# RWKV attention with a mixture of experts behind it: the first expert's weight pieces are requested by two engines in turn, and the state of six units is faded by TensorE

## The chip, the core and the metric

The kernel runs on one core of one Trainium2 chip. A core has a matrix engine (TensorE, called PE in the profile), a vector engine (VectorE, DVE), a scalar engine (ScalarE, ACT), a general engine (GpSimd, POOL), an engine that mostly issues transfers (SyncE, SP), and 16 DMA engines. PE, DVE, ACT, POOL and SP each run their own list of instructions in order and wait for one another by semaphores. The metric is the time of one execution in microseconds (us) on the chip; smaller is better.

## The reference

Attention first, for 4 batches, 8 heads, 768 tokens and a head width of 48; then a mixture of 8 experts on the 3072 tokens of 384 numbers that come out of it, each token going to the one expert with the highest logit.

```python
for t in range(S):                                   # S = 768
    kt, vt, rt = k[:, :, t], v[:, :, t], r[:, :, t]
    cur = np.einsum('bhd,bhe->bhde', u[None] * kt, vt)
    y[:, :, t] = np.einsum('bhd,bhde->bhe', rt, state + cur)
    state = w[None, :, :, None] * state + np.einsum('bhd,bhe->bhde', kt, vt)
...
logits = x @ w_gate + modality_bias[modality_id]     # x: 3072 x 384
e_idx = np.argmax(logits, axis=1)
...
for e in range(E):                                   # E = 8
    h = np.maximum(x[mask] @ w1[e], 0.0)             # 384 x 1024
    out[mask] = gate_w[mask, None] * (h @ w2[e])     # 1024 x 384
```

## The kernel before

**Units.** The attention is cut into 24 units: chunk c = 0 to 5 of 128 tokens, and in each chunk the batches b = 0 to 3; unit i is `c*4 + b`. The decay w is taken out by powers (`rc`, `kc`, `kt` are r and k multiplied by powers of w). For a unit, `scores` makes the 128x128 score blocks of the 8 heads on PE, `causal` masks them on DVE into `at`, and `values` puts into one PSUM bank `py` the product of r with the state `st` that the earlier chunks left (L396) and the product of `at` with v (L403). Into a second bank, `pst`, it puts the unit's own contribution to the state, k times v (L410), and the eight numbers per token by which v itself enters (`bonus`, L341). There is one bank for `pst`, so the next unit's L410 waits until the last reader of the bank has finished. The scales of the expert weights (`pww`, below) use the same bank.

**The state.** The state of a batch after a chunk is the state before, multiplied row by row by w to the 128th power, plus the contribution in `pst`. The multiplication is done by `fade` on ACT (L384: two 112x192 activations in a step, for two batches and half of the head pairs), into the other of two state buffers; the addition by `state` on DVE (L444: two additions in a step, for the upper and the lower half of the rows). Both are done one step apart per unit.

**The step loop.** One loop of 23 steps writes the program out by hand. Step i works on several units at a time: PE's `scores(i+1)`; DVE's `token(i-1)` (`py` plus `dv`, L418), followed by ACT's square of the row (L433); `taken(i)` (DVE copies the eight numbers to `d`); `state(i-1)`; the `begin` hooks; POOL's sends of rows (L580), `decay` (POOL `rc`, L313), `carry` (POOL `kt`, L320), DVE's `kc` (L332); the row's scale on DVE; `own(i, 0)` on ACT, four of the eight activations v times d into `dv` (L354); `high(i-1)` on ACT (L456); `causal(i+1)` on DVE (L374); `own(i, 1)` on ACT, the other four; `low(i-1)` on DVE (L460); `flip(i-1)`, a transposing transfer that SP issues (L465); `values(i)` on PE; `fade` on ACT; and the `at` hooks. POOL's `own_keys` (L325, `rk`) is written at a step's start.

Ahead of `scores(i)` for units 1 to 13 stand `DENSE` = 6 matmuls of 128x512 on constant data (L362), whose result is overwritten.

**The first expert.** Its weights (W1 and W2 together, 3 MB in float32) come in six pieces of 128x1024 (`raw`, 512 KB each, L824), all issued by SP: piece 0 at the end of step 8, 1 and 2 at the end of step 9, 3 and 4 at the end of step 10, 5 at the end of step 11. The constant `O` is 8. SP reads the expert's number with `value_load` ahead of piece 0. For each piece ACT makes the sum of squares (`norm`, L827): piece 0 at the end of step 9, pieces 1 and 2 at the end of step 10, 3 and 4 at the end of step 11, 5 at the end of step 12. From pieces 0 to 2 comes the scale of W1 (`scales("w1")`: a small PE matmul L841 into `pww`, then DVE from L844 on) at the beginning of step 11; from pieces 3 to 5 that of W2 at the beginning of step 13. `split` makes of a piece its high half in float16 on ACT (`whi`, L857) and the rest on DVE (`wlo`, L862): piece 0 at the end of step 11, 1 and 2 at the end of step 12, 3 to 5 at the end of step 13. The experts' matmuls (L916 up, L990 down) begin at the end of step 12, between the attention's; after step 23 the other experts follow.

Since every engine's list is in order, a `norm` that waits for its piece holds up all that ACT has behind it, and the PE matmul of a scale that waits for a `norm` holds up all of PE's list.

## Time and profile before

| | |
|---|---|
| three runs | 365.92, 362.83, 364.58 us; median 364.58 |
| the profiled execution | 365.14 us, of which the span from first to last instruction is 363.3 |
| PE busy | 337.2 us, 93% of the span |
| DVE, ACT, POOL busy | 230.3, 178.2, 167.2 us |
| mean granted clock of PE | 0.968 |
| mean DMA rate over the span | 138 GB/s |

The profile is a record of one execution. Times in it are microseconds from the start of the span. "L827" is line 827 of the kernel before; the kernel of the change has other line numbers, up to 32 higher. In a line of the timeline the first number is the start, the second the busy time, then the engine, the line, the operation, the tiles (out <- in), their sizes, and how many instructions were put together (x4); in square brackets stands how long the engine had been idle ahead of it and what it waited for. A record of the windows gives for a stretch of time the busy time of each engine with its number of instructions, the granted clock of PE as a share of full speed (PEclk), the mean busy share of the DMA engines, and their rate. One PE matmul of the program in float32 shows as two records.

In this kernel the steps 8 to 13 lie at about 52 to 106 us.

### The profile page before, as it was taken

To read this page: it belongs to the slowest core of one execution; us is meant where nothing else is said; L and a number is where in the kernel's file an instruction comes from. 1 tells how busy PE (TensorE), PEld (TensorE's weight loads), DVE (VectorE), ACT (ScalarE), POOL (GpSimd) and SP (SyncE) were. 2 spreads that over 40 slices of the span, in tenths; PEclk is the share of its full clock that TensorE was granted. 3 is DMA by queue.
4 is the path that set the end of the run, shared out by engine and by line. 5 is a ranking of instruction groups with operands and counts; after the bars stand their busy time and mean duration, and the time that the engine had idled before them with its cause. 6 is when DMAs were issued, how large, how long until landed. Compare 5 with 4: busy or idle time off the path is not lost. (4 is left out here: it accounts for less than half of the span.)

```text
span 363.3 us, 14983 instructions
## 1 busy us (share of the span) xinstructions
PE 337.2 (93%) x5387; PEld 265.1 (73%) x5387; DVE 230.3 (63%) x762; ACT 178.2 (49%) x479; POOL 167.2 (46%) x229
## 2 busy tenths in 40 slices
PE   7799999869799999999999899997999999999893
PEld 3577778557788787988977677775677888777661
DVE  7867999979797977596558632349432323323950
ACT  7467874778656566566432122245122222256711
POOL 7996867845436673444165511136111121111731
PEclk9899999958799999999999999999999999999998
DMA  6988997998957998863354631125922212112120
GB/s 179 270 212 167 202 241 201 296 289 180 234 124 151 215 242 258 176 133 85 87 110 153 242 69 43 43 43 164 232 65 56 52 43 62 46 22 65 22 56 5
DMA packets 60749, 50.29 MB, mean 138 GB/s; under 512 B 46872, under 2 KB 54311, under 8 KB 60448
## 3 DMA queue, kind: packets, MB, share of 16 engines
q1 hardware_dynamic: 57504, 40.21, 49.8%
q0 software_dynamic: 3200, 9.47, 7.1%
q8 instruction: 30, 0.49, 0.6%
q14 instruction: 15, 0.12, 0.1%
HBM read 28.39 MB, written 11.83 MB: 111 GB/s over the span
## 5 line engine op out<-in xcount | busy, mean ns | idle before, releaser
L916 PEld LDWEIGHTS <-whi 128*128 128x128 f16 x1248 | 73.6, 99 | 3.7 <-issue 0.9
L990 PEld LDWEIGHTS <-hh 128*128 128x128 f16 x416 | 38.0, 98 | 32.9 <-ACT hh L920 8.0
L916 PE MATMUL phb<-mxT,whi 128*128 128x128 f16 x768 | 50.8, 219 | 0.0
L354 ACT ACTIVATE dv<-kv,d 128x48 f32<-128x48 f32 x192 | 47.9, 323 | 4.8 <-DVE d L346 2.8
L325 POOL TENSOR_TENSOR rk<-rc,kc 128x512 f32<-128x512 f32 x24 | 30.6, 1275 | 40.0 <-DVE posi L554 13.5
L920 ACT ACTIVATE hh<-phb 128x256 f16<-128x256 f32 (+1 forms) x48 | 21.3, 454 | 42.0 <-PE L990 13.7
L916 PEld LDWEIGHTS <-wlo 128*128 128x128 f16 x624 | 38.2, 99 | 3.2 <-DVE wlo L862 3.2
L925 DVE SCALAR_TENSOR_TENSOR hl<-phb,hh 128x256 f16<-128x256 f32 (+1 forms) x48 | 24.2, 511 | 24.7 <-ACT hh L920 14.5
L374 DVE TENSOR_TENSOR at<-psc,mask 128x512 f32<-128x512 f32 x48 | 31.6, 683 | 4.5 <-PE psc L368 4.3
L313 POOL TENSOR_TENSOR rc<-ud,powr 128x512 f32<-128x512 f32 (+1 forms) x27 | 31.8, 1184 | 2.7 <-PE py L396 1.5
L1000 DVE TENSOR_SCALAR fac<-mt,wf 128x1 f32<-128x1 f32 x17 | 3.6, 212 | 45.5 <-ACT otb L876 39.0
L916 PE MATMUL phb<-mxT,wlo 128*128 128x128 f16 x384 | 30.0, 219 | 2.6 <-DVE wlo L862 2.6
L995 PEld LDWEIGHTS <-hl 128*128 128x128 f16 x208 | 19.3, 97 | 14.7 <-issue 3.1
L876 ACT ACTIVATE otb<-po,fac 128x384 f32<-128x384 f32 x16 | 9.2, 577 | 42.2 <-PE phb L916 42.2
L990 PE MATMUL po<-wlo,hh 128*128 128x384 f16 x136 | 28.0, 326 | 1.7 <-DVE wlo L862 1.7
L580 POOL DMA_INDIRECT rows<-row,posi x24 | 24.1, 1006 | 11.6 <-DVE base L556 3.6
L990 PE MATMUL po<-whi,hh 128*128 128x384 f16 x136 | 28.3, 327 | 1.0 <-ACT hh L920 1.0
L885 POOL TENSOR_TENSOR seenb<-otb,putb 128x1 int32<-128x1 int32 x16 | 5.0, 310 | 52.8 <-ACT otb L876 50.0
L368 PEld LDWEIGHTS psc<-rc,kc 64*64 64x64 f32 (+1 forms) x768 | 21.5, 136 | 9.8 <-issue 4.8
L916 PE MATMUL phs<-mxT,whi 128*128 128x128 f16 x432 | 28.5, 224 | 0.0
L368 PE MATMUL psc<-rc,kc 64*64 64x128 f32 (+1 forms) x768 | 27.6, 280 | 0.9 <-issue 0.7
L403 PE MATMUL py<-kv,at 128*64 128x48 f32 x768 | 28.0, 229 | 0.0
(255 smaller groups left out, 673.7 us busy)
## 6 DMA issues: line engine op xcount, KB each, us to landing
ud<-in_pd SPq DMA_DIRECT2D x24, 384.0 KB
kv<-in_pt SPq DMA_DIRECT2D x24, 384.0 KB
raw<-in_w SPq DMA_DIRECT2D x12, 512.0 KB
raw<-in_w SPq DMA_DIRECT2D x2, 1536.0 KB, 6.3
rows<-pad SPq DMA_DIRECT2D x10, 193.0 KB
rows<-row,posi POOLq DMA_INDIRECT x24
xT<-row SPq DMA_TRANSPOSE x23
xn<-rows SPq DMA_TRANSPOSE x17
```

Of the source, the lines that this page charges most:

```text
L313: nc.gpsimd.tensor_mul(u["rc"][:, s], u["rT"][:, s], self.powr[:, s])
L325: nc.gpsimd.tensor_mul(u["rk"], u["rc"], u["kc"])
L354: nc.scalar.activation(u["dv"][:, sl], u["v"][:, sl], AF.Copy, scale=u["d"][:, h : h + 1])
L368: nc.tensor.matmul(u["ps"][j][s, pr * P : (pr + 1) * P], u["kc"][r, pr, s], u["rc"][r, pr, :], start=True, stop=True)
L374: nc.vector.tensor_mul(u["at"][:, j * NPR : (j + 1) * NPR, :], u["ps"][j].rearrange("p (q t) -> p q t", q=NPR), self.mask.unsqueeze(1).to_ ...
L403: nc.tensor.matmul(py[t, sl], u["at"][:, j * NPR + pr, t], u["v"][:, sl], start=c == h == 0, stop=h == H - 1, skip_group_check=True)
L580: i = nc.gpsimd.indirect_dma_start(out=self.rows, out_offset=bass.IndirectOffsetOnAxis(ap=u["posi"][:, b : b + 1], axis=0), in_=u["row"][: ...
L916: self.nc.tensor.matmul(ph[:, q * P : (q + 1) * P], w[:, c0 : c0 + P], self.xT[:, xq, t * P : (t + 1) * P], start=i == q == 0, stop=i == l ...
L920: self.nc.scalar.activation(self.hh[:, f0 : f0 + fb, t * P : (t + 1) * P], p3, AF.Relu)
L925: self.nc.vector.scalar_tensor_tensor(self.hl[:, f0 : f0 + fb, r], p3, 0.0, self.hh[:, f0 : f0 + fb, r], ALU.max, ALU.subtract)
L990: self.nc.tensor.matmul(po[:, :DM], self.hh[:, f, t * P : (t + 1) * P], w[:, c0 : c0 + DM], start=n == q == f == 0, stop=False)
L995: self.nc.tensor.matmul(po[:, :DM], self.hl[:, f, t * P : (t + 1) * P], self.whi[:, c0 : c0 + DM], start=False, stop=f == FB - 1)
```

## The change

Four edits come together.

- **The pieces.** The even pieces are issued by SP, one at the end of each of the steps 8, 9 and 10. The odd ones are issued by ACT, one in the middle of each of the steps 9, 10 and 11 (a new hook, `mid`, behind `high` and ahead of `causal`), with a `value_load` of the expert's number on ACT ahead of piece 1. The squares are spread: 1, 3 and 5 in the middle of steps 10, 11 and 12 and 0, 2 and 4 at the end of steps 9, 10 and 11.
- **The state of units 8 to 13** (`FADED`). ACT's `fade` and DVE's two additions are left out for them. Instead PE multiplies the old state by a diagonal matrix `wd` with w to the 128th power (four float32 matmuls of 112x112 on 112x96), into the bank `pst`, and L410 adds the unit's contribution on top. ACT copies the sum out of the bank in one 112x384 copy (`settled_state`), in the next step behind the row's square. The matrices are made once, by four activations on ACT in the setup.
- **Half of d times v for units 9 to 13** (`SHARED`). The second four of ACT's eight activations become one multiplication of 128x192 on POOL.
- **Fewer constant matmuls.** Ahead of `scores` of units 9 to 13 stand two, not six.

The core of the diff:

```diff
+FADED = range(8, 14)
+SHARED = range(9, 14)
...
+        self.wd = c.tile([P, NPR, 112], F32, name="wd")
+        for pr in range(NPR):
+            nc.scalar.activation(self.wd[:112, pr, :], self.id32[:112, :112], AF.Copy, scale=self.w128[:112, pr : pr + 1])
+            yield
...
     def own(self, i, q):
+        if q and i in SHARED:
+            half = lambda t: t[:, DM // 2 :].rearrange("p (h e) -> p h e", e=D)
+            nc.gpsimd.tensor_mul(half(u["dv"]), half(u["v"]), u["d"][:, H // 2 :].unsqueeze(2).to_broadcast([P, H // 2, D]))
+            return
...
-            for q in range(DENSE):
+            for q in range(2 if i - 1 in FADED else DENSE):
                 nc.tensor.matmul(u["ps"][q % 2], self.ones16, self.warm, start=True, stop=True)
...
     def fade(self, c, bs, prs):
+        if c * B + bs.start in FADED:
+            return
...
     def values(self, i):
+        faded = i in FADED
+        if faded:
+            for pr in range(NPR):
+                nc.tensor.matmul(pst[:112, pr * 2 * D : (pr + 1) * 2 * D], self.wd[:112, pr, :], st[:112, b, pr, :], start=pr == 0, stop=False, skip_group_check=True)
...
-                nc.tensor.matmul(pst[HALVES[j], sl], u["kt"][:, pr, HALVES[j]], u["v"][:, sl], start=True, stop=True)
+                nc.tensor.matmul(pst[HALVES[j], sl], u["kt"][:, pr, HALVES[j]], u["v"][:, sl], start=not faded, stop=not faded or h == H - 1, skip_group_check=faded)
...
     def state(self, i, j):
+        if i in FADED:
+            return
...
+    def settled_state(self, i):
+        if i in FADED:
+            b, c = self.units[i]
+            self.nc.scalar.copy(self.st[(c + 1) % 2][:112, b].rearrange("p a e -> p (a e)"), self.ctx_[i]["pst"][:112, :DM])
...
+        def beside(q):
+            if q == 1:
+                self.eida = nc.scalar.value_load(self.ctl[:, :1], min_val=0, max_val=E - 1)
+            self.load(self.eida, NQ, q, eng=nc.scalar)
...
-            plan(O + (q + 1) // 2, first(q))
+            if q % 2 == 0:
+                plan(O + q // 2, first(q))
...
-        plan(O + 2, norm(1))
+        mid[O + 1] = lambda: beside(1)
+        mid[O + 2] = lambda: (beside(3), self.norm(junk, 1))
+        mid[O + 3] = lambda: (beside(5), self.norm(junk, 3))
+        mid[O + 4] = norm(5)
         plan(O + 2, norm(2))
...
-        plan(O + 3, norm(3))
         plan(O + 3, norm(4))
...
-        plan(O + 4, norm(5))
...
             each(i, self.taken) if i else None
+            each(i - 1, self.settled_state)
...
             each(i - 1, self.high)
+            mid.get(i, lambda: None)()
```

How the instructions stand on three engines, before and after. First ACT, from the end of step 9 to the beginning of step 11; `junk` is the result of a `norm`, `row,ssq` of the row's square, `row<-py,sx` of `high`. Before:

```order
L827 ACTIVATE junk,wssq<-raw 128x1024
L433 ACTIVATE row_1311,ssq_1313<-py_1363 128x384
L354 ACTIVATE dv_1486<-kv_901,d_1467 128x48 x4
L456 ACTIVATE row_1311<-py_1363,sx_1314 128x384
L354 ACTIVATE dv_1486<-kv_901,d_1467 128x48 x4
L384 ACTIVATE st_93<-st_92,w_183 112x2x96 x2
L827 ACTIVATE junk,wssq<-raw 128x1024 x2
L433 ACTIVATE row_1311,ssq_1313<-py_1507 128x384
```

The same place with the change:

```order
L850 ACTIVATE junk,wssq<-raw 128x1024
L449 ACTIVATE row_1308,ssq_1310<-py_1366 128x384
L469 COPY st_93<-pst_1391 112x384
L364 ACTIVATE dv_1485<-kv_906,d_1467 128x48 x4
L479 ACTIVATE row_1308<-py_1366,sx_1311 128x384
L847 ISA
L847 DMA raw<-in_w 128x1024
L850 ACTIVATE junk,wssq<-raw 128x1024 x2
L449 ACTIVATE row_1308,ssq_1310<-py_1505 128x384
```

Four of the eight `dv` activations and the two of `fade` have gone, and a copy out of `pst` (behind the square that stands behind piece 0's `norm`) and the request for piece 3 have come in.

SP from piece 0 to pieces 3 and 4, the ends of steps 8 to 10; `ud` and `kv` are the inputs of later units, `xT` the transposes of `flip`. Before:

```order
L824 DMA raw<-in_w 128x1024
L298 DMA ud_86<-in_pd 96x1024
L305 DMA kv_1282<-in_pt 128x2x384
L465 DMA_TRANSPOSE xT_1312<-row_1311 128x6x128
L824 ISA
L824 DMA raw<-in_w 128x1024
L824 ISA
L824 DMA raw<-in_w 128x1024
L298 DMA ud_87<-in_pd 96x1024
```

With the change:

```order
L847 DMA raw<-in_w 128x1024
L304 DMA ud_86<-in_pd 96x1024
L311 DMA kv_1283<-in_pt 128x2x384
L488 DMA_TRANSPOSE xT_1309<-row_1308 128x6x128
L847 ISA
L847 DMA raw<-in_w 128x1024
L304 DMA ud_87<-in_pd 96x1024
```

Behind the transpose stands one request, for piece 2, where there were two, for pieces 1 and 2; piece 1 is now in ACT's list.

PE in step 9, from the product with the old state into the bank `pst`, with what an instruction waits for. Before:

```order
L396 MATMUL py_1363<-st_92,rc_939 64x96 [waits DVE_49]
L396 MATMUL py_1363<-st_92,rc_939 64x96 x7
L403 MATMUL py_1363<-kv_770,at_1199 64x48 [waits DMAHW5_49]
L403 MATMUL py_1363<-kv_770,at_1199 64x48 x15
L410 MATMUL pst_1388<-kv_770,kt_89 64x48 [waits DVE_49,PE_49]
```

With the change:

```order
L408 MATMUL py_1366<-st_92,rc_944 64x96 [waits DVE_49]
L408 MATMUL py_1366<-st_92,rc_944 64x96 x7
L415 MATMUL py_1366<-kv_775,at_1198 64x48 [waits DMAHW5_49]
L415 MATMUL py_1366<-kv_775,at_1198 64x48 x15
L421 MATMUL pst_1391<-st_92,wd 112x96 [waits Activation_49]
L421 MATMUL pst_1391<-st_92,wd 112x96 x3
L426 MATMUL pst_1391<-kv_775,kt_89 64x48
```

L410 (now L426) wrote first into the bank and waited for DVE's additions of the unit before; now L421 writes first and waits for ACT's copy.

More of the change, by code (lines that the diff above doesn't have):

```diff
@@ L818, in pads, with load @@
                 tc.declare_no_dep(i.ins, group="first", reason="not the first place's rows")
-    def load(self, eid, n, *qs):
+    def load(self, eid, n, *qs, eng=None):
         for q in qs:
             sl = slice(q * 2 * WC // n, (q + 1) * 2 * WC // n)
-            self.nc.sync.dma_start(self.raw[:, sl], self.w12[bass.ds(eid, 1), :, sl].rearrange("o p c -> (o p) c"))
+            (eng or self.nc.sync).dma_start(self.raw[:, sl], self.w12[bass.ds(eid, 1), :, sl].rearrange("o p c -> (o p) c"))
     def norm(self, junk, q):
@@ L1027, in run @@
         fills = []
-        at, begin = {}, {}
+        at, begin, mid = {}, {}, {}
         def plan(step, f):
```

## The prediction

> **What bounds the kernel now.** The page first: how busy each engine is.
>
> ```profile
> span 363.3 us, 14983 instructions
> PE 337.2 (93%) x5387; PEld 265.1 (73%) x5387; DVE 230.3 (63%) x762; ACT 178.2 (49%) x479; POOL 167.2 (46%) x229
> ```
>
> PE works 337.2 of 363.3 us, so the time falls only where PE idles, where its work is slow, or where it has work that can go. Next the waits of PE between 50 and 130 us, the stretch that the change touches, longest first (total, times, longest):
>
> ```profile
> PE pww L841 <- ACT junk L827: 4.6, 1, 4.6
> PE pww L841 <- DVE st L444: 2.3, 1, 2.3
> PE pst L341 <- issue: 0.6, 2, 0.4
> ```
>
> These are the matmuls of the two scales: W1's waits 4.6 us for ACT's squares of the pieces, W2's waits 2.3 us for DVE's additions to the state, which hold the one `pst` bank; the third row is a gap of 0.4 us in step 12, used below. Then the windows, with PE's granted clock as the third number from the end:
>
> ```profile
> 61.00:67.00 6.00, 6.00 (x158) 4.91 (x156) 5.86 (x26) 3.43 (x13) 3.96 (x4) 1.00 0.89 227
> 67.00:70.00 3.00, 2.98 (x66) 2.15 (x61) 2.97 (x7) 2.64 (x9) 2.25 (x3) 1.00 1.24 215
> 70.00:72.00 2.00, 1.32 (x34) 0.86 (x32) 2.00 (x9) 1.85 (x7) 2.00 (x3) 1.00 1.00 394
> 74.00:76.00 2.00, 0.07 (x1) 0.00 (x0) 0.00 (x0) 1.27 (x3) 0.00 (x0) 0.54 1.74 232
> 76.00:78.00 2.00, 2.00 (x31) 1.97 (x30) 1.80 (x9) 1.69 (x8) 0.50 (x1) 0.50 0.71 234
> 78.00:80.00 2.00, 2.00 (x45) 2.00 (x44) 2.00 (x4) 2.00 (x8) 2.00 (x3) 0.50 0.99 393
> 80.00:82.00 2.00, 2.00 (x30) 1.43 (x29) 2.00 (x5) 1.97 (x4) 0.97 (x2) 0.50 1.05 296
> 84.00:86.00 2.00, 2.00 (x56) 1.83 (x54) 1.94 (x9) 1.30 (x6) 0.71 (x1) 0.90 0.57 121
> 94.00:106.00 12.00, 12.00 (x189) 10.73 (x188) 10.29 (x23) 8.42 (x21) 5.66 (x5) 0.72 0.88 221
> 106.00:160.00 54.00, 53.21 (x1102) 44.73 (x1100) 42.06 (x145) 32.03 (x102) 29.26 (x33) 1.00 0.82 184
> ```
>
> After each wait the clock is halved for a while: 0.50 from 76 to 82, 0.72 on the mean of 94 to 106. From 94 on PE is never idle (12.00 of 12.00, then 53.21 of 54). So the end moves by as much as W2's matmul moves, plus what PE's own work and clock do behind it. Ahead of 94 the timeline says which engine sets the pace; PE first.
>
> ```profile
> 75.93 0.16 PE L841 MATMUL pww<-wssq,onesb 128*128 128x3 bf16 x1 [4.62 <-ACT junk L827]
> 76.03 1.55 PE L396 MATMUL py<-st,rc 112*64 112x96 f32 x16
> 81.13 2.72 PE L362 MATMUL psc<-warm 128*128 128x512 f16 x6
> 85.10 0.88 PE L396 MATMUL py<-st,rc 112*64 112x96 f32 x16
> 89.36 1.51 PE L916 MATMUL phs<-mxT,whi 128*128 128x128 f16 x24
> 90.71 0.83 PE L916 MATMUL phs<-mxT,wlo 128*128 128x128 f16 x12
> 93.88 0.17 PE L841 MATMUL pww<-wssq,onesb 128*128 128x3 bf16 x1 [2.34 <-DVE st L444]
> ```
>
> The same sixteen matmuls take 1.55 us at the half clock and 0.88 at the full one, a factor of 1.76. PE is through with step 12 at 91.54 (90.71 + 0.83) and waits. DVE in the same stretch:
>
> ```profile
> 76.14 0.16 DVE L844 TENSOR_REDUCE wtotw<-pww 128x1 f32<-128x3 f32 x1 [2.55 <-PE pww L841]
> 77.52 1.30 DVE L518 TENSOR_TENSOR oh<-er,mr 128x32 f16<-128x32 f32 x1
> 83.33 0.33 DVE L444 TENSOR_TENSOR st<-st,pst 64x192 f32<-64x192 f32 x1
> 83.81 0.36 DVE L444 TENSOR_TENSOR st<-st,pst 48x192 f32<-48x192 f32 x1
> 92.49 0.55 DVE L418 TENSOR_TENSOR py<-py,dv 128x384 f32<-128x384 f32 x1
> 93.03 0.71 DVE L444 TENSOR_TENSOR st<-st,pst 64x192 f32<-64x192 f32 x2
> ```
>
> It starts with W1's scale and has no idle time to speak of up to 93.74. Before the change, then, the chain is: piece 2 lands, ACT squares it, W1's scale, 17.6 us of DVE, W2's scale, and PE from there on.
>
> **The change, part by part.** *The pieces.* ACT's squares, and SP's requests:
>
> ```profile
> 66.81 1.06 ACT L827 ACTIVATE junk<-raw 128x1024 f16<-128x1024 f32 x1 [1.77 <-DMA raw<-in_w]
> 70.16 1.00 ACT L354 ACTIVATE dv<-kv,d 128x48 f32<-128x48 f32 x4
> 71.06 0.79 ACT L384 ACTIVATE st<-st,w 112x192 f32<-112x192 f32 x2
> 72.05 1.06 ACT L827 ACTIVATE junk<-raw 128x1024 f16<-128x1024 f32 x1 [0.20 <-DMA raw<-in_w]
> 74.73 1.06 ACT L827 ACTIVATE junk<-raw 128x1024 f16<-128x1024 f32 x1 [1.53 <-DMA raw<-in_w]
> 60.80 0.38 SPq L824 DMA_DIRECT2D raw<-in_w  x1
> 67.03 0.93 SPq L824 DMA_DIRECT2D raw<-in_w  x2
> ```
>
> All three squares wait for their data. Piece 1 is requested at 67.03 now, behind a transpose; from ACT, behind `high` of step 9 and the new `value_load`, it goes out some 3 us sooner, and piece 2 has one piece less ahead of it. The request and the `value_load` stand where ACT idles (1.77 us ahead of 66.81, and the 0.79 and 1.00 of `fade` and half of `dv` go too), so they cost nothing; without that cover, their own length, under 2 us. How much sooner piece 2 lands no row shows. Lower end nothing: the DMA engines are full from 61 to 76 (shares 0.89, 1.24, 1.00), the same bytes must pass, and piece 3, now requested ahead of the squares of pieces 1 and 2 and no longer behind them, shares with piece 2. Upper end 2.7 us: piece 2 in the place of piece 1, its square at 72.05 and not at 74.73. I take half, **1.3**, since 61 to 67 moved 227 GB/s and 70 to 72, almost only pieces, 394: the early stretch has some room, but not all of it.
>
> On this place bears a rule of the Trainium skill, page "DMA: Bandwidth & Descriptors", section "Issuing engines are not separate DMA queues": transfers from different engines run on the same 16 DMA engines, and issuing from several saves only the time of issuing. By it piece 2 would land as before, and this term be about nothing, as in rival 2 below; the shares near 1.00 agree.
>
> *State off DVE.* Two additions (0.33 + 0.36) leave step 12; those at 93.03 too. W2's matmul then waits for ACT: square of the row, copy. Rows for these:
>
> ```profile
> 93.12 0.49 ACT L433 ACTIVATE row<-py 128x384 f16<-128x384 f32 x1 [2.37 <-issue]
> L167 ACT COPY wtok<-pwk 128x384 f32<-128x384 f32 x1 | 0.5, 478 | 1.5 <-PE pwk L166 1.5
> ```
>
> So 0.49 + 0.48 + 0.1 for the accumulator behind `token` where it was 0.15 + 0.71: +0.2. DVE's side of W2 moves by -1.3 - 0.7 + 0.2 = -1.8. Queued behind that copy on ACT are `dv` and `high`, at most 0.5 us later, with idle time there. In step 10 the copy out of the bank stands behind the square of piece 0, which ends at 67.96; with the row's square the bank is free at about 69.0, where L410 of that step ran at
>
> ```profile
> 67.60 0.85 PE L410 MATMUL pst<-kv,kt 128*64 128x48 f32 x16
> ```
>
> PE then idles 1.4 us there; that comes out of the 4.6 us it waits later, as does whatever the four setup activations and the earlier steps shift, as long as W1's scale stays later than about 72.
>
> *Half of `dv` on POOL.* A multiplication of half the size of POOL's `kt`, so 0.6 us each.
>
> ```profile
> 77.50 1.27 POOL L325 TENSOR_TENSOR rk<-rc,kc 128x512 f32<-128x512 f32 x1 [4.53 <-DVE mr L515]
> 90.26 1.22 POOL L320 TENSOR_TENSOR kt<-kv,wtok 128x384 f32<-128x384 f32 x1
> ```
>
> In step 12 it ends at 91.48 + 0.6 = 92.1, ahead of `token` at 92.49: hidden, with 0.4 to spare; without cover, 0.6. Beside POOL's `rk` a small DVE operation took 1.30, so I add +0.3 to DVE for two more such multiplications (ends 0 and 1.2). DVE's side: **-1.5**.
>
> *PE's own work.* `wd` adds eight records in a unit where L396 has sixteen: 0.44 at the full clock, 0.8 at the half one (up to half as much again for the wider weights). The four constant matmuls that go save 1.8 us in step 12 (4/6 of 2.72). In steps 8 to 11 they make gaps that end in the wait.
>
> *The clock.* From 76 to 82 PE was 2.00 of 2.00 busy with small float32 matmuls and stayed at 0.50; it came back (0.90 at 84 to 86) after the six at 81.13. With two, I take it to stay halved until the next large float16 run, the expert's L916. The Trainium skill, page "TensorE: Matmul & The Clock Gate", Part 1, says a busy window of about 3.4 us lifts the halving whatever the instructions. By it the cut costs nothing and rival 1 would come out. Six busy microseconds at 0.50 speak against it.
>
> PE's side of W2, then: from 91.54, -1.3 (W1 sooner), -1.8 (constants), +0.8 + 0.8 (`wd` of units 11 and 12), +5.1 for the work between the clock's return and 91.54 (0.90 on the mean of 84 to 86 puts the return at 84.4; 7.1 us less the gap of 0.4 are 6.7, at a factor of 1.76), -0.9 if L916 lifts the clock midway (half of 2.34 x 0.76): 94.2. That is later than DVE's 92.4, so W2's matmul comes at 94.2, **+0.3**, without a wait ahead of it. With no wait there is no second halving: 94 to 106 at a clock of 0.72 lost 12 x 0.28 = 3.4 us; I take back **2.4**, since the first may reach into it. `wd` of unit 13: **+0.4**. Sum +0.3 - 2.4 + 0.4 = **-1.7**. From the profiled 365.14 (span 363.3 and 1.84 around it) that is 363.4; the median of the three runs is 0.56 below that execution, so the forecast is **362.9**.
>
> **Rivals.**
> 1. *The clock comes back as before*, from two constant matmuls. For it: the two still are 0.9 us of large work. W2 is then set by DVE at -1.5, the wait and the second halving remain, +0.8 for `wd`: -0.7, 363.9.
> 2. *The pieces land no sooner.* For it: the full shares. Then 1.3 of the forecast is lost: 364.2.
> 3. *Neither long halving*: W1's wait split in two gaps (1.4 and about 2) and W2's wait gone. Against it: PE idles from 71.3 (1.32 busy from 70 on), and 74 to 76 is at 0.54, so about 3 us of idleness were enough for a drop, hardly more than a gap of this rival. It would give rival 1 with the 3.4 back: -4.1, 360.5.
> 4. *Slower: the halved clock holds through step 13.* If L916's 36 matmuls do not lift it, W2 comes at 95.1 (+1.2) and step 13 runs halved as before with +0.8 for `wd`: +2.0, 366.6. It decides at L916 of step 12; one more halved stretch of the same kind behind it (half of 3.4) gives 368.3.
>
> That the change does not do what it says is possible for the requests alone: the copy that ACT runs ahead of them waits for `token`. That is rival 2.
>
> **How the numbers follow.** Forecast 0.38, rival 1 0.20, rival 2 0.14, rival 3 0.15, rival 4 0.13. A measurement can tell about 1%, 3.65 us. Below 360.9: rival 3, a tail of 0.05 of the forecast with piece 2 at its upper end (1.4 more): 0.20. Above 368.2: the further stretch of rival 4 and a price of POOL's contention at its end: 0.07. The rest, 0.73, is within. The range reaches from rival 3 with a little left out, 360.0, to rival 4, 366.8.
>
> **What would show it.** Piece 2's square ahead of 74.7 and W1's matmul at 73 to 75 (first term). No DVE additions in steps 9 to 14, the bank released by ACT. The clock between 84 and 90 at 0.50 (forecast) or near 1.00 (rivals 1 and 3), and the wait ahead of W2's matmul gone or not. POOL's `dv` ahead of `token` in step 12; if `token` waits for POOL, that term is wrong. The forecast fails if W1's matmul comes later than 76, or if the clock stays halved past 98.

## The result: 0.6% slower, and the profile after

The changed kernel takes 366.73 us in the median of 17 runs (365.13 to 370.03), the kernel before 365.19 in 17 runs beside them: a ratio of 1.0058 with a 95% interval of 1.0036 to 1.0081. On the chip of e5 to e12 it was 1.0072 (1.0035 to 1.0109). So it is slower by about 2 us, where the forecast was 1.7 us less.

One thing must be known before the trace is read. The profiled execution of the changed kernel took 365.13 us, the lowest of its 17 times, and that of the kernel before 365.14, about its median. The two traces end together (spans 363.2 and 363.3). They show where the change lost and where it won, but not the loss of a typical run; for its size the timed experiments count. Four profiled executions of the experiments (e1, e7, e12, e17) were longer than most runs of their kernel; of them only distances within the execution are used. The page, first its span and busy times:

```profile
span 363.2 us, 15003 instructions
PE 336.3 (93%) x5415; PEld 266.7 (73%) x5415; DVE 228.6 (63%) x750; ACT 172.6 (48%) x457; POOL 172.0 (47%) x234
```

The waits of PE around the change, as before in total, times and longest:

```profile
PE pww L864 <- ACT st L469: 8.7, 2, 6.0
PE pst L421 <- ACT st L469: 0.3, 1, 0.3
```

Before, W1's matmul waited 4.6 us for ACT's square and W2's 2.3 us for DVE's addition. Now both wait for the same new instruction, `st L469`, ACT's copy of the settled state out of the bank, and longer: 8.7 us together instead of 6.9. ACT and the requests in the timeline show what stands in front of it:

```profile
61.12 0.38 SPq L847 DMA_DIRECT2D raw<-in_w  x1
66.29 0.39 SPq L847 DMA_DIRECT2D raw<-in_w  x1
63.48 0.40 ACTq L847 DMA_DIRECT2D raw<-in_w  x1
68.47 0.34 ACTq L847 DMA_DIRECT2D raw<-in_w  x1
66.22 1.06 ACT L850 ACTIVATE junk<-raw 128x1024 f16<-128x1024 f32 x1 [2.87 <-DMA raw<-in_w]
71.84 1.06 ACT L850 ACTIVATE junk<-raw 128x1024 f16<-128x1024 f32 x1 [2.26 <-DMA raw<-in_w]
76.16 1.06 ACT L850 ACTIVATE junk<-raw 128x1024 f16<-128x1024 f32 x1 [3.18 <-DMA raw<-in_w]
77.22 0.47 ACT L449 ACTIVATE row<-py 128x384 f16<-128x384 f32 x1
77.68 0.47 ACT L469 COPY st<-pst 112x384 f32<-112x384 f32 x1
```

Requests: pieces 0 and 2 by SP at 61.12 and 66.29, pieces 1 and 3 by ACT at 63.48 and 68.47. Piece 1 is asked for 3.5 us sooner than before, yet its square begins at 71.84 (72.05 before); and piece 2's square begins at 76.16, where it was 74.73. Behind that square stand the row's square and the copy, which ends at about 78.1. Then PE, with the matmuls by `wd` between the two scales:

```profile
78.20 0.16 PE L864 MATMUL pww<-wssq,onesb 128*128 128x3 bf16 x1 [6.02 <-ACT st L469]
81.45 1.33 PE L421 MATMUL pst<-st,wd 112*112 112x96 f32 x8
87.31 1.02 PE L421 MATMUL pst<-st,wd 112*112 112x96 f32 x8
95.85 0.17 PE L864 MATMUL pww<-wssq,onesb 128*128 128x3 bf16 x1 [2.71 <-ACT st L469]
```

W1's matmul begins at 78.20 (75.93 before, +2.27): 1.43 from the piece and 0.84 from the copy, since it now follows the square's start by 2.04 us and not by 1.20. W2's is at 95.85, +1.97. The windows of that stretch, with the clock third from the end, and then `token` of units 11 to 14 on DVE:

```profile
78.00:80.00 2.00, 1.80 (x25) 1.71 (x26) 1.53 (x9) 1.23 (x7) 0.24 (x1) 0.50 1.39 190
80.00:82.00 2.00, 2.00 (x33) 1.91 (x30) 2.00 (x4) 2.00 (x4) 2.00 (x2) 0.50 1.02 358
82.00:84.00 2.00, 2.00 (x50) 1.89 (x49) 2.00 (x5) 1.71 (x3) 1.23 (x2) 0.97 1.01 319
98.00:100.00 2.00, 2.00 (x31) 1.90 (x28) 2.00 (x4) 2.00 (x5) 1.85 (x2) 0.70 1.10 289
106.00:160.00 54.00, 53.95 (x1100) 45.13 (x1098) 43.21 (x150) 33.50 (x108) 29.32 (x33) 1.00 0.78 184
```

```profile
84.96 0.55 DVE L434 TENSOR_TENSOR py<-py,dv 128x384 f32<-128x384 f32 x1
94.27 0.55 DVE L434 TENSOR_TENSOR py<-py,dv 128x384 f32<-128x384 f32 x1
105.58 0.55 DVE L434 TENSOR_TENSOR py<-py,dv 128x384 f32<-128x384 f32 x1
111.56 0.56 DVE L434 TENSOR_TENSOR py<-py,dv 128x384 f32<-128x384 f32 x1
```

From W1's matmul to `token` of unit 12 the changed kernel needs 16.07 us (16.56 before), to `token` of unit 14 33.36 (34.79 before). So behind W1 it is the quicker one, by 0.5 and 1.4 us; it starts 2.3 us later. Of that lag 0.84 us are left at unit 14, and none at the end of this execution.

### The profile page after: what moved, and what is told of

It is laid out like the page before. It is cut to its first block, busy times and chain, and to the rows that moved or that the text cites. A ratio compares the mean times of both kernels' runs of the same rounds, so it can differ in the third digit from the quotient of the medians.

```text
span 363.2 us, 15003 instructions
## 1 busy us (share of the span) xinstructions
PE 336.3 (93%) x5415; PEld 266.7 (73%) x5415; DVE 228.6 (63%) x750; ACT 172.6 (48%) x457; POOL 172.0 (47%) x234
## 5 line engine op out<-in xcount | busy, mean ns | idle before, releaser
L939 PEld LDWEIGHTS <-whi 128*128 128x128 f16 x1248 | 72.4, 98 | 3.8 <-issue 0.9
L939 PE MATMUL phb<-mxT,whi 128*128 128x128 f16 x768 | 50.8, 219 | 0.0
L331 POOL TENSOR_TENSOR rk<-rc,kc 128x512 f32<-128x512 f32 x24 | 30.6, 1275 | 31.4 <-DVE posi L577 10.5
L364 ACT ACTIVATE dv<-kv,d 128x48 f32<-128x48 f32 x172 | 43.0, 324 | 3.5 <-issue 1.9
L939 PEld LDWEIGHTS <-wlo 128*128 128x128 f16 x624 | 37.8, 98 | 3.7 <-DVE wlo L885 3.7
L319 POOL TENSOR_TENSOR rc<-ud,powr 128x512 f32<-128x512 f32 (+1 forms) x27 | 33.4, 1240 | 2.3 <-DMA ud<-in_pd 1.5
L939 PE MATMUL phb<-mxT,wlo 128*128 128x128 f16 x384 | 30.0, 219 | 2.6 <-DVE wlo L885 2.6
L603 POOL DMA_INDIRECT rows<-row,posi x24 | 25.4, 1058 | 11.6 <-issue 3.9
L415 PEld LDWEIGHTS py<-kv,at 128*64 128x64 f32 x768 | 27.1, 146 | 0.9 <-issue 0.3
L885 DVE SCALAR_TENSOR_TENSOR wlo<-raw,ws,whi 128x1024 f16<-128x1024 f32 (+1 forms) x18 | 27.1, 1551 | 0.8 <-ACT whi L880 0.8
```

The source lines that it names most:

```text
L319: nc.gpsimd.tensor_mul(u["rc"][:, s], u["rT"][:, s], self.powr[:, s])
L331: nc.gpsimd.tensor_mul(u["rk"], u["rc"], u["kc"])
L364: nc.scalar.activation(u["dv"][:, sl], u["v"][:, sl], AF.Copy, scale=u["d"][:, h : h + 1])
L415: nc.tensor.matmul(py[t, sl], u["at"][:, j * NPR + pr, t], u["v"][:, sl], start=c == h == 0, stop=h == H - 1, skip_group_check=True)
L603: i = nc.gpsimd.indirect_dma_start(out=self.rows, out_offset=bass.IndirectOffsetOnAxis(ap=u["posi"][:, b : b + 1], axis=0), in_=u["row"][: ...
L885: self.nc.vector.scalar_tensor_tensor(self.wlo[:, sl], self.raw[:, sl], sc, self.whi[:, sl], ALU.mult, ALU.subtract)
```

## The experiments

Three kinds of number are used. The ratio is that of the times against the kernel before on the same chip, with its 95% interval. "p2" is the distance from SP's request for piece 0 to the start of piece 2's square in the profiled execution, "W1" the distance from that start to W1's matmul; both lie within one execution, so that a shift of the whole step drops out. e12 shows why: in that profile of the kernel before W1's matmul is at 79.83, 3.9 us later than in the first, but both distances are the same to 0.1 us. The runs e1 to e4, e5 to e12, e13 to e16 and e17 with e18 come from four chips; ratios from different chips are compared with less certainty.

| kernel | state on PE | pieces | half of dv on POOL | ratio (95%) | p2 | W1 |
|---|---|---|---|---|---|---|
| before | none | old | no | 1 | 13.93 | 1.20 |
| changed | 8 to 13 | new | yes | 1.0058 (1.0036, 1.0081) | 15.04 | 2.04 |
| e8, changed again | 8 to 13 | new | yes | 1.0072 (1.0035, 1.0109) | 14.49 | 2.04 |
| e12, before again | none | old | no | 1.0015 (0.9980, 1.0049) | 13.84 | 1.20 |
| e1 | none | new | no | 1.0070 (1.0029, 1.0112) | 14.60 | 1.20 |
| e2 | 8 to 13 | old | no | 1.0060 (1.0030, 1.0091) | 13.44 | 2.04 |
| e3 | none | old | yes | 1.0005 (0.9964, 1.0045) | 13.49 | 1.20 |
| e4 | 8 to 13 | new, 3 late | yes | 1.0155 (1.0088, 1.0222) | 13.58 | 2.04 |
| e5 | 8 to 13, early copy | old | no | 1.0022 (0.9987, 1.0057) | 13.07 | 1.20 |
| e6 | 8 to 13, early copy | old | yes | 1.0122 (1.0075, 1.0169) | 14.00 | 1.20 |
| e7 | 8 to 13, early copy | new | yes | 1.0050 (1.0014, 1.0085) | 15.46 | 1.20 |
| e9 | 8, 9, 12, 13 | old | no | 0.9994 (0.9965, 1.0023) | 12.92 | 1.20 |
| e10 | 10, 11 | old | no | 1.0064 (1.0028, 1.0100) | 13.86 | 2.04 |
| e11 | none | 1 by ACT | no | 1.0009 (0.9983, 1.0035) | 13.14 | 1.20 |
| e13 | none | 1, 3 by ACT | no | 0.9992 (0.9959, 1.0024) | 12.61 | 1.20 |
| e14 | none | new | yes | 1.0022 (0.9990, 1.0054) | 12.62 | 1.20 |
| e15 | 8, 9, 12, 13 | old | yes | 0.9975 (0.9931, 1.0019) | 13.53 | 1.20 |
| e18, e15 again | 8, 9, 12, 13 | old | yes | 0.9968 (0.9928, 1.0007) | 13.71 | 1.20 |
| e16 | 8, 9, 12, 13 | new | yes | 1.0024 (0.9980, 1.0068) | 14.46 | 1.20 |
| e17 | 8, 9, 12, 13 | new, 3 by SP | yes | 1.0047 (1.0010, 1.0085) | 13.29 | 1.20 |

### The parts alone: e1 to e4

Two theories of the loss came first: T1 puts it down to the requests, since piece 3 takes a share of the DMA engines from piece 2, T2 to the state on PE. e1 has the edit of the pieces alone, e2 the state alone (with the fewer constant matmuls, which hang on `FADED`), e3 half of `dv` on POOL alone; e4 is the changed kernel with a later request for piece 3:

```diff
# e1:  FADED = range(0); SHARED = range(0)
# e2:  SHARED = range(0); requests and squares as before
# e3:  FADED = range(0); requests and squares as before
# e4:
-        mid[O + 2] = lambda: (beside(3), self.norm(junk, 1))
+        mid[O + 2] = norm(1)
         plan(O + 2, norm(2))
+        plan(O + 2, lambda: beside(3))
```

> The kernel before with only the edit of the pieces: odd ones requested by ACT, squares spread; the state, dv and the constant matmuls as before. Theory T1 (the requests cost: piece 3, now under way beside piece 2, takes a share of the DMA engines, as in the changed kernel, where piece 2's square began at 76.16 and not at 74.73): piece 2's square at 75.5 to 76.5, the matmul of W1's scale 1 to 2 us later than the 75.93 of before, the time 0.3 to 0.6% above the kernel before. Theory T2 (the loss comes from the state on TensorE, the pieces are harmless): piece 2 no later than 75, time within 0.2% or below.

> The kernel before with only the state edit: units 8 to 13 faded by TensorE, settled by one ACT copy, two constant matmuls instead of six; pieces and dv as before. T1: about the time of the kernel before, between 0.3% less and 0.2% more (DVE has 0.7 us less to do before W2's scale, PE has 1.0 us more per unit and 1.8 less in step 12). T2: 0.4 to 0.8% above the kernel before, since wd takes 1.0 to 1.3 us a unit where 0.4 to 0.8 was reckoned and W2's scale waits for the ACT copy.

> The kernel before with only half of dv of units 9 to 13 on POOL. T1 and T2 alike: within 0.2% of the kernel before; ACT has 1.0 us less per step, but waits for its pieces anyway. If POOL's multiplications cost DVE more than 1 us in steps 9 to 13, 0.3% above.

> The changed kernel with the request for piece 3 moved behind the square of piece 2 on ACT, nothing else. T1: piece 2 has the DMA engines to itself and its square begins at 74.7 or sooner, W1's matmul 1.5 to 2.5 us earlier than the 78.20 of the changed kernel, the time 0.3 to 0.6% below the changed kernel, at most 0.2% above the kernel before (the square of piece 3 may then wait in step 11). T2: piece 2 sooner or not, the time stays 0.4 to 0.8% above the kernel before.

Both e1 (+0.7%) and e2 (+0.6%) are slower; e3 is not. So neither theory is the whole: T1 did not allow for the state alone to cost, T2 not for the pieces. The trace of e2 gave a third theory. Its timeline at W1, ACT first, then PE:

```profile
75.09 1.06 ACT L850 ACTIVATE junk<-raw 128x1024 f16<-128x1024 f32 x1 [0.74 <-DMA raw<-in_w]
76.15 0.47 ACT L449 ACTIVATE row<-py 128x384 f16<-128x384 f32 x1
76.61 0.47 ACT L469 COPY st<-pst 112x384 f32<-112x384 f32 x1
77.13 0.16 PE L864 MATMUL pww<-wssq,onesb 128*128 128x3 bf16 x1 [4.13 <-ACT st L469]
```

The matmul of W1's scale puts its result into the one bank that `pst` of unit 10 still holds. Before, DVE's additions had emptied it by 73.4 us, long ahead of piece 2's square. Now the copy empties it, and in ACT's list that stands behind the squares of pieces 1 and 2 and the row's square: W1 follows the square by 2.04 us instead of 1.20. This is theory T3.

In e1 the bank is not the matter (W1 follows the square by 1.20), but the squares in the middle of a step hold up what ACT has behind them:

```profile
79.44 0.57 DVE L430 TENSOR_TENSOR py<-py,dv 128x384 f32<-128x384 f32 x1 [1.51 <-ACT dv L360]
89.17 1.28 DVE L881 SCALAR_TENSOR_TENSOR wlo<-raw,ws,whi 128x1024 f16<-128x1024 f32 x1 [1.03 <-ACT whi L876]
```

`token` of unit 10 waits 1.51 us for `dv`, whose second half stands behind the square of piece 1; but W1's matmul comes only at 82.48, for piece 2, so this wait is hidden. The second one is not. The first split `whi` stands behind the square of piece 3 and the second half of `dv`, `wlo` waits for it, and W1's matmul to `token` of unit 11 takes 7.9 us, where it is 6.8 in the kernel before and in the changed one.

In e4 piece 2 came sooner (p2 13.58 against 15.04 and 14.49 in the changed kernel), as T1 expected, but the time rose to +1.6%. What the late request did in step 11:

```profile
75.44 0.35 ACTq L847 DMA_DIRECT2D raw<-in_w  x1
79.18 0.34 ACTq L847 DMA_DIRECT2D raw<-in_w  x1
84.33 1.06 ACT L850 ACTIVATE junk<-raw 128x1024 f16<-128x1024 f32 x1 [4.71 <-DMA raw<-in_w]
85.39 1.13 ACT L880 ACTIVATE whi<-raw,ws 128x1024 f16<-128x1024 f32 x1
```

Piece 3, requested at 75.44, holds up its square until 84.33, with ACT idle for 4.71 us; and behind that square, which the change put into the middle of step 11, stands the first split `whi`, which DVE waits for ahead of `token`. W1's matmul to `token` of unit 11 took 10.5 us there, 6.8 in the changed kernel. The wait was only moved.

### The bank: e5, e7, e9, e10 (and e6, e8)

In e5, e6 and e7 the copy is written one place earlier, directly behind `values`; e8 is the changed kernel again, as a reference.

```diff
-            each(i - 1, self.settled_state)     # at the step's start
...
             self.values(i)
+            each(i, self.settled_state)
```

> The kernel with only the state edit, but ACT's copy of the state out of the bank is written directly behind values of the same step, ahead of the squares of the pieces, so that the bank is free before ACT waits for a piece. Theory T3 (the copy behind the squares keeps the bank and so W1's and W2's matmuls, which use the same bank: in the state-only kernel W1's matmul began 2.04 us after piece 2's square began, before it was 1.20): 1.2 us after the square, the wait of W2's matmul about 1 us shorter, the time 0.3 to 0.6% below the state-only kernel, within 0.2% of the kernel before. Theory T2 (wd's own PE work is the cost): W1's matmul sooner all the same, but the time still 0.4 to 0.8% above the kernel before.

> The changed kernel with the pieces requested and squared as before and the copy directly behind values; the state on TensorE, half of dv on POOL, two constant matmuls remain. T1 and T3 together (requests and bank were the two losses): at most the time of the kernel before, 0.4% less to 0.1% more. T2: 0.4 to 0.8% above the kernel before.

> The changed kernel with the copy directly behind values, pieces as in the change. T3 with T1: W1's matmul 1.2 us after piece 2's square began (2.04 in the changed kernel), the square itself as late as there; the time 0.2 to 0.5% below the changed kernel on this chip, still 0.2 to 0.6% above the kernel before. If T1 is wrong and only the bank mattered: no slower than the kernel before.

> The changed kernel itself, unchanged, on the chip of these runs, as the point of reference: 0.4 to 0.8% above the kernel before if the parts overlap, up to 1.3% if the losses of the pieces alone (0.7%) and of the state alone (0.6%) add up.

In e5, e6 and e7 W1's matmul is back at 1.20 us behind the square. e5 (1.0022) lies below e2 (1.0060), and e7 (1.0050) below e8 (1.0072), but the intervals overlap. e8 itself loses no more than the pieces or the state alone, so the two losses do not add up. The early copy has a price of its own, and e6 at +1.2% was a miss. It is not explained in full; the mean granted clock of its timed runs was 0.967, that of the kernel before beside them 0.976. The timeline of ACT in e5, step 11:

```profile
83.94 0.48 ACT L469 COPY st<-pst 112x384 f32<-112x384 f32 x1 [3.69 <-PE pst L347]
84.32 1.15 ACT L880 ACTIVATE whi<-raw,ws 128x1024 f16<-128x1024 f32 x1
85.37 1.05 ACT L850 ACTIVATE junk<-raw 128x1024 f16<-128x1024 f32 x1
```

In step 11 the copy now waits 3.69 us for PE, and `whi` and the squares of pieces 3 and 4 wait behind it; W1's matmul to `token` of unit 11 took 9.7 us in e5 and e6, against 6.8. A test without that price moves nothing, but takes the units that matter out of the edit:

```diff
# e9:   -FADED = range(8, 14)   +FADED = (8, 9, 12, 13)      (as e2 otherwise)
# e10:  -FADED = range(8, 14)   +FADED = (10, 11)
```

> The state edit for units 8, 9, 12 and 13 only; units 10 and 11 are faded by ACT and added by DVE as before (their constant matmuls stay six); pieces and dv as before. Theory T3 (what the state edit loses is the bank: unit 10's copy stands behind the squares that wait for pieces, and W1's matmul behind the copy): W1's matmul 1.2 us after piece 2's square began, as before, and the time within 0.25% of the kernel before. Theory T2 (wd's PE work, 1.0 to 1.3 us a unit, is the loss): four of six units, so about 0.4% above the kernel before.

> The state edit for units 10 and 11 only, the counterpart. T3: W1's matmul 2.0 us after piece 2's square began, the time 0.2 to 0.6% above the kernel before. T2: two of six units, 0.2% above at most.

This rules out T2. Four of the six units on PE cost nothing that can be measured (0.9994, 0.9965 to 1.0023), where T2 expected 0.4%; the two units 10 and 11 alone cost as much as all six (1.0064, 1.0028 to 1.0100), where T2 allowed 0.2%. The squares and W1's matmul of e9, then of e10:

```profile
73.95 1.06 ACT L850 ACTIVATE junk<-raw 128x1024 f16<-128x1024 f32 x1 [0.90 <-DMA raw<-in_w]
75.15 0.16 PE L864 MATMUL pww<-wssq,onesb 128*128 128x3 bf16 x1 [2.58 <-ACT junk L850]
```

```profile
75.47 1.06 ACT L850 ACTIVATE junk<-raw 128x1024 f16<-128x1024 f32 x1 [1.25 <-DMA raw<-in_w]
76.99 0.47 ACT L469 COPY st<-pst 112x384 f32<-112x384 f32 x1
77.51 0.16 PE L864 MATMUL pww<-wssq,onesb 128*128 128x3 bf16 x1 [6.05 <-ACT st L469]
```

The releaser of W1's matmul is the square in e9 and the copy in e10, as in the changed kernel. That the units 10 and 11 carry the loss of the state edit is shown; that all of it (0.6% are 2.3 us) is the 0.84 us of the bank at W1 is not. The copy of unit 11 and W2's later matmul are in e10 too, and its profile has a wait of 2.46 us for a transfer, `mxT`, the experts' input, which e9 and the changed kernel have not. And `FADED` moves the constant matmuls along: ahead of `scores` of units 11 and 12, just before W1's wait, stand two in e10 and six in e9. PE then waits 6.05 us for W1 in e10 and 2.58 in e9, and the mean granted clock of the timed runs was 0.973 in e10, 0.979 in e9 and 0.976 in the kernel before. Against the clock as the cause speaks e2: the same loss at 0.975 beside 0.976. The constant matmuls were not tried by themselves.

### The pieces: e11, e13, e14, e16, e17

```diff
# e11: before, with
+        mid[O + 1] = lambda: beside(1)                    # piece 1 by ACT, nothing else
# e13: as e11, with
+        mid[O + 2] = lambda: beside(3)                    # piece 3 by ACT too, squares as before
# e14: the edit of the pieces, FADED = range(0), SHARED = range(9, 14)
# e16: the changed kernel, FADED = (8, 9, 12, 13)
# e17: as e16, with
-        mid[O + 2] = lambda: (beside(3), self.norm(junk, 1))
+        mid[O + 2] = norm(1)                              # piece 3 by SP, ahead of 4
```

> The kernel before with only piece 1 requested by ACT in the middle of step 9; pieces 2 to 5, the squares, the state and dv as before. T1 (piece 2 loses its share to piece 3, requested too soon, not to piece 1): piece 2's square 13.0 to 13.9 us after piece 0's request (13.9 before, 14.5 to 15.5 with all the pieces edited), the time at or up to 0.3% below the kernel before. If it is the second queue itself that costs: 14.5 us or more and 0.3 to 0.7% above.

> The kernel before itself, for a profile on the chip of these runs: the same time within 0.4%; piece 2's square 13 to 14 us after piece 0's request, W1's matmul 1.2 us behind the square's start. If W1's and W2's matmuls lie as far apart from its first profile as they do between kernels (2 us), single profiles can't carry the comparison.

> The kernel before with pieces 1 and 3 requested by ACT in the middle of steps 9 and 10; piece 5, the squares, the state and dv as before. T1: piece 2's square 14.4 to 15.5 us after piece 0's request (13.1 with piece 1 alone by ACT, 12.9 to 14.0 in six kernels with the old order), the time 0.2 to 0.6% above the kernel before. If the squares' new places are what cost in the edit of the pieces: within 0.2% of the kernel before.

> The edit of the pieces with half of dv on POOL, the state as before, so that no dv stands behind the spread squares. T1: piece 2's square 14.4 to 15.5 us after piece 0's request, W1's matmul 1.2 us behind it, the time 0.2 to 0.6% above the kernel before. If the squares ahead of dv were the loss of the pieces-only kernel (0.7%): within 0.2% of the kernel before.

> The changed kernel with units 10 and 11 faded by ACT and added by DVE as before. T3: W1's matmul 1.2 us behind piece 2's square. T1 and T3 together: half of the loss of 0.6 to 0.7% stays, the time 0.1 to 0.5% above the kernel before. If the bank was all: within 0.2%.

> The changed kernel with units 10 and 11 as before (as in the run before) and the request for piece 3 with SP's for piece 4 at the end of step 10; pieces 1 and 5 by ACT, squares as in the change. If the early request for piece 3 delays piece 2 (T1 in its narrower form: it does so when it goes out 2 us behind piece 2's request): piece 2's square 12.6 to 13.8 us after piece 0's request (14.46 with ACT's request), the time 0.3% below to 0.2% above the kernel before. If ACT's request for piece 1 delays it: 14.4 us or more, 0.1 to 0.5% above.

Piece 1 by ACT alone changes nothing (e11). T1 in its plain form falls with e13 and e14: they ask for piece 3 early too, and piece 2 comes sooner than ever (12.6; e1's 14.60 had spoken for it and does not fit). e13 says more. It has e1's requests for pieces 1 and 3, but the squares at their old places, and its ratio is 0.9992 where e1's is 1.0070. So with the state as before it is the squares' new places that cost (or the request for piece 5, the other difference), not those two requests. In e14, with half of `dv` out of ACT's list, 1.0022 are left. The requests of e14 and of e16:

```profile
65.11 0.40 ACTq L843 DMA_DIRECT2D raw<-in_w  x1
67.89 0.54 SPq L843 DMA_DIRECT2D raw<-in_w  x1
71.09 0.34 ACTq L843 DMA_DIRECT2D raw<-in_w  x1
74.59 1.06 ACT L846 ACTIVATE junk<-raw 128x1024 f16<-128x1024 f32 x1 [0.90 <-DMA raw<-in_w]
```

```profile
63.97 0.40 ACTq L847 DMA_DIRECT2D raw<-in_w  x1
66.49 0.60 SPq L847 DMA_DIRECT2D raw<-in_w  x1
68.69 0.34 ACTq L847 DMA_DIRECT2D raw<-in_w  x1
76.07 1.06 ACT L850 ACTIVATE junk<-raw 128x1024 f16<-128x1024 f32 x1 [2.60 <-DMA raw<-in_w]
```

In e14 ACT asks for piece 3 3.2 us after SP asked for piece 2, and piece 2's square starts 6.7 us after its request. In e16, and in the changed kernel, the request follows after 2.2 us, and piece 2 takes 9.6 (9.9 in the changed kernel). What brings the request forward is DVE more than ACT. In e14 `high`, which stands ahead of the request, waits 1.86 us for DVE, where unit 9's two additions and a `kc` of 2.21 us stand in that step. In e16 there are no additions, and `kc` takes 0.68. (It takes 0.7 in every profile with units 8 and 9 on PE and 2.2 in all the others; the cause was not tried.)

With the state edit in place and only this request moved, piece 2 came sooner both times: 15.04 and 14.49 to 13.58 (e4), 14.46 to 13.29 (e17). So in part the edits of the pieces and of the state work against each other: relieving DVE and ACT brings piece 3's request forward into piece 2's transfer. It is not the whole difference to e14, though. In e4 and e17 piece 2 still took 8.3 and 8.2 us from its request, with piece 3 asked for only 8.5 and 5.6 us behind it. The rest goes with units 8 and 9 on PE, where piece 2 itself is asked for sooner behind piece 0 (after 4.9 to 5.4 us, elsewhere 5.8 to 6.5); that was not tried by itself.

Yet the time did not follow: e17 was still 0.5% above, where at most 0.2% was expected, and no better than e16 (1.0024, on another chip). Its profile has the wait of e4 in small: piece 3's square waits 1.89 us in the middle of step 11, ahead of `whi`, and W1's matmul to `token` of unit 11 takes 7.6 us and not 6.8. e14 shows the same, with a wait of 1.01 us and 7.5 us.

```profile
83.07 1.06 ACT L850 ACTIVATE junk<-raw 128x1024 f16<-128x1024 f32 x1 [1.89 <-DMA raw<-in_w]
84.12 1.13 ACT L880 ACTIVATE whi<-raw,ws 128x1024 f16<-128x1024 f32 x1
```

### The version to which they point: e15 and e18

```diff
# requests and squares as before; SHARED = range(9, 14)
+FADED = (8, 9, 12, 13)
```

> Half of dv on POOL and the state edit for units 8, 9, 12 and 13, pieces requested and squared as before: the version to which T1 and T3 point. 0.4% below to 0.1% above the kernel before.

> The candidate (half of dv on POOL, state on TensorE for units 8, 9, 12 and 13, pieces as before) a second time: 0.5% below to 0.2% above the kernel before; both sets together tell whether it is faster by more than 0.2%.

0.9975 (0.9931 to 1.0019) and 0.9968 (0.9928 to 1.0007): below the kernel before both times, by about 1 us, and below the changed kernel by 0.8 to 1.0% (ratio of the ratios, across chips). Against the kernel before each interval still holds 1, so a gain is possible and not shown; in e18 it may lie in the granted clock, which was 0.983 on the mean and 0.974 in the kernel before beside it (e15: 0.976 and 0.977). e17, run beside e18 on the same chip, differs from it by the pieces alone and is 0.8% above it (1.0047 against 0.9968).

## Why the prediction was wrong, step by step

Two terms on the way to W1's matmul failed: the bank at W1 was missing, and the pieces had the wrong sign. The gain from the clock did not come either; most other terms held.

- **What bounds the kernel** was read rightly: W1's and W2's matmuls, then PE without a gap. What was missed stands in the same row: "hold the one `pst` bank" was said of W2's matmul alone. **W1's matmul uses the same bank.** The prediction worked out the late copy for unit 9 in step 10 (an idle of 1.4 us for PE; the profile has none there) and hid it under W1's wait, and took the ACT copy of unit 12 at +0.2 for W2 (measured: W2's matmul 1.58 us behind `token`, before 1.39, so +0.19). The copy of unit 10, between the two, sets W1 itself: +0.84, a term that the sum lacked, on the path that the whole sum was about. With the pieces' +1.43 it puts W1's matmul at 78.20, later than the 76 that the prediction named as a sign of failing. e9 and e10 show that the units 10 and 11 carry the loss of the state edit; how much of it is this wait stays open, as said above.
- **The pieces**: -1.3 was taken as half of the span from 0 to -2.7. It was +1.4 in the first profile (by p2 +1.1, in e8 +0.6), outside the span. The prediction named the rival (piece 3 shares with piece 2) but set the lower end at nothing, since "the same bytes must pass". Piece 2 can land later all the same when the next piece is under way beside it: with only that request moved back it came 0.9 to 1.5 us sooner (e4, e17). The rule of the Trainium skill, page "DMA: Bandwidth & Descriptors", section "Issuing engines are not separate DMA queues" (transfers of all issuing engines run on the same 16 engines and interleave), was the better guide; the trace agrees, as piece 1, asked for 3.5 us sooner, was squared 0.2 sooner, and piece 2 later. e11 agrees too: issuing from a second engine alone is worth nothing (1.0009).
- **The squares' new places** had no term of their own in the sum. In the middle of a step they stand ahead of `whi`, and of the second half of `dv` where ACT makes it: W1's matmul to `token` of unit 11 took 7.9 us in e1, 7.5 in e14, 7.6 in e17 and 10.5 in e4, against 6.8. In the changed kernel it is 6.8, since piece 3 is there in time; the price of that is piece 2's delay. e1 against e13 speaks for these places as the loss of the pieces' edit when the state is as before.
- **DVE's side**, -0.7 + 0.3 between W1 and `token` of unit 12: -0.49 measured. Right as a sum; of its parts, -0.7 is -0.73 in e2, and e3 shows nothing of the +0.3 (16.56 us as before).
- **`wd` on PE** was reckoned at 0.44 us a unit at the full clock (up to half as much again for the wider weights), after L396's duration for half as many records; it takes 1.02 (1.33 partly halved). The size was off by a factor of two, but e9 shows that for four of the six units this cost nothing that can be measured.
- **Half of `dv` on POOL**: hidden, as said (e3, 1.0005). The place was not: in step 12 it ran at 85.84, just behind the copy of d, 8 us ahead of `token`.
- **The clock**: the forecast had the halving last through step 12 for want of constant matmuls, and took 2.4 us back because no second one would follow. In the first profile the halving ended at 82, 3.9 us behind W1's matmul, with small float32 matmuls only (0.97 from 82 to 84, the two constant ones stand at 84.02), and a second one came behind W2's wait; that is rival 1, and the -2.4 did not come. This execution agrees with the Trainium skill, page "TensorE: Matmul & The Clock Gate", Part 1, by which a busy window of about 3.4 us lifts the halving, whatever number of matmuls fills it. e8 does not. It went more as forecast: PE was busy and halved from 77.56 until about 89.4, deep into step 12 though not up to L939 (93.14), with no second halving behind W2. The windows of e8:

```profile
78.00:80.00 2.00, 2.00 (x36) 2.00 (x34) 1.97 (x8) 1.23 (x5) 0.87 (x1) 0.50 0.76 238
82.00:84.00 2.00, 2.00 (x33) 1.83 (x33) 2.00 (x4) 1.07 (x3) 0.59 (x1) 0.50 1.07 374
88.00:90.00 2.00, 2.00 (x46) 2.00 (x42) 1.97 (x8) 2.00 (x4) 1.76 (x2) 0.65 1.21 132
96.00:98.00 2.00, 1.54 (x43) 1.45 (x44) 1.23 (x6) 1.31 (x6) 0.16 (x1) 1.00 0.65 169
```

  So the same program does either, and a term of -2.4 should not rest on which. Nor was it a gain where it came: W1's matmul to `token` of unit 14 took 34.60 us in e8, 33.36 in the first profile. The mean granted clock was 0.975 in the changed kernel's timed runs and 0.976 in those of the kernel before beside e8, so the cut of the constant matmuls shows no effect on it.
- **From W2 to the end one to one**: not so in the profiles. The lag of 0.84 us at unit 14 was gone at the end of the first one. Rival 4, the only slower one, had another cause (the clock) than the one that came.

What stays open: how the 2 us of a typical run divide between the bank, the pieces and the clock. The two profiles of the changed kernel are each the quickest of their runs; the first shows 2.3 us lost at W1, which it has won back by its end. And which part of the pieces' edit costs in e17 was not tried by itself.

## What to carry over

Before an engine is given the job of emptying a shared PSUM bank, list every user of that bank, not only the next one in the loop, and ask what stands ahead of the emptying instruction in that engine's list: here two squares that wait for transfers. A request for a transfer moved forward can delay the one under way, here by 0.9 to 1.5 us; so when an engine that issues transfers is relieved, look again at when its requests go out. And where single profiles of one program differ by as much as the forecast, as the halved clock did here, take the size from timed runs and only the order of events from the trace.

## What the runs showed of the hardware that was not expected

- A 512 KB piece took 9.5 to 9.9 us from its request to its consumer when the next piece was requested by another engine 2.0 to 2.2 us behind it (the changed kernel, e8, e16). With that request 5.6 and 8.5 us behind and the state still on PE it took 8.2 to 8.3 (e17, e4). With the state as before it took 6.3 to 6.7, though the next request came 2.8 to 3.2 us behind (e13, e14), and 8.7 in e1. So the distance of the two requests does not set it alone.
- Eight records of float32 matmuls with 112x112 weights on 112x96 took 1.02 us (L421), sixteen with 112x64 weights on the same 0.88 (L396): 0.128 against 0.055 us each, though the weights are less than twice as wide.
- With nothing but small float32 matmuls behind W1's own the halved clock was lifted within 4 us in one execution (the changed kernel, 78.2 to 82.1) and not in the 4.8 us from 76.0 to 80.8 in another (the kernel before). In e8 11.8 us of unbroken PE work ran at 0.50.
